# The first expert's raw w1 blocks 4 to 7, loaded behind the first queries into the buffers of the sums acc

## The chip, the cores and the metric

The kernel runs on one core of a Trainium2 chip. The metric is the device time of one execution in microseconds (us), the median of three runs. TensorE (PE) multiplies, VectorE (DVE), ScalarE (ACT) and GpSimd (POOL) work on tiles, and SyncE (SP) issues every DMA. Each of the five runs its own list of instructions in a fixed order, and an instruction that waits holds up all behind it on its engine.

## What is computed

A sparse attention over 4 batches, 8 heads and 768 positions of 64 numbers feeds a mixture of 4 experts. Each query sees the keys closer than 16 positions, and besides these 24 summaries of blocks of 32 (maximum of the keys, mean of the values).

```
k_sum = k.reshape(B, H, nb, block, D).max(axis=3)
v_sum = v.reshape(B, H, nb, block, D).mean(axis=3)
a = softmax([mask(scale * q @ k.T), scale * q @ k_sum.T + log(block)])
x = a @ concat(v, v_sum)                      # 3072 tokens of 512
h = np.maximum(x @ w1[e], 0.0)                # w1[e]: 512 x 1024
out += p[:, e:e + 1] * (h @ w2[e])            # w2[e]: 1024 x 512, p: probabilities of the domains
```

## The kernel before

**Tiles.** The 3072 tokens are eight blocks `tb` of 384. A block's attention is eight pieces `n` (96 queries times four heads). Pieces 0 to 7 make block 0 and have a path of their own, `first_tokens`, whose order is written out by hand with the keys `KEYS` and `STEPS`. From piece 8 on, a piece is: `load_piece` (its keys `kr` and its queries and values `qv`), `stage_a` (high and low parts: `ks`, `qs`, `v12`, `v3`), `scores` (`psc` on PE, its maxima on DVE, exponentials on ACT, in `ms`), `probs` (`rs`, `ms`, `aw`), `transposed` (a DMA that transposes `aw` into `awT`), `values` (`px` on PE, for two pieces one after the other) and `to_x` (`xh` on ACT, `xl` on DVE). Pieces 8 to 15 make block 1, and `xl` of pieces 14 and 15 is the last that block 1 waits for.

**Batches.** Pieces 16 and up belong to batch 1. For these `setup_k(1)` loads four chunks `kch1_0` to `kch1_3`, of which DVE takes block maxima into `ksr1`; `spread_k` then copies `ksr1` to `ks1` with four small DMAs. `setup_v(1)` does the same with `vch1_0` to `vch1_3` and sums `vsr1`, out of which ACT (`vs5`), PE (`pvs1`) and DVE make the summaries of the values. All eight chunks share two buffers (`chunk`), so that chunk 2 can be loaded only when DVE is through with chunk 0, and so on.

**Experts.** A block runs `plain_units`: for each of the eight 128-wide blocks `fc` of w1, 12 matmuls `ph` of 384 columns (`mm1`), then `hh` (ACT) and `hl` (DVE), and at the end the products `po` with w2 (`mm2`), 72 matmuls of 512 columns for a block of tokens, added to `acc` on DVE. A raw weight block of 256 KB is loaded to a buffer `wr`, ACT casts it to the high part (`wh` for w1), and POOL subtracts for the low part (`wl`); for w2 of the first expert DVE does (`w`), and the split w2 is stored to DRAM (`wd`) for later. Block 0 goes through experts 0 and 1, then block 1 through experts 1 and 0, and the rest follows. In names such as wr10_4, the digits are the 1 of w1, the expert, and `fc`.

**What sets the order.** In `first_tokens` engines keep the program's order. Behind that a scheduler places instructions by its own estimate of time. SP's list is one queue: a DMA whose buffer is not yet free, or whose data are not yet written, holds up all later DMAs.

**Buffers that the change touches.** `wr` has four buffers (lines 657 to 660). Before, w1 blocks 0 to 3 and then w2 blocks 0 to 3 of expert 0 take them in turn. w1 blocks 4 and 5 are asked for at the end of the hand-written list (key 99.0, lines 633 and 634), and so stand on SP behind the four stores of split w2, and behind the release of `wr` by the first splits of w2; blocks 6 and 7 are loaded when `plain_units` asks for them. `acc` (line 770) has six buffers of the same size; the first is written when the first product `po` of block 0 is done.

Of the kernel before, what the change touches and what calls it, by code (L numbers as in the profile page):

```python
# [8 lines left out]
F32 = mybir.dt.float32  # L9
# [7 lines left out]
P = 128  # L17
# [12 lines left out]
FC = DF // P  # L30
# [32 lines left out]
def attn_moe(ctx: ExitStack, tc: tile.TileContext, qvL, qv0, v0L, kD, kT, vT, w1L, w2L, dpL, cst, out):  # L63
# [21 lines left out]
    def pool(name, bufs=1, **kw):  # L85
        return ctx.enter_context(tc.tile_pool(name=name, bufs=bufs, **kw))
# [7 lines left out]
    sb = pool("sb")  # L94
# [302 lines left out]
    def first_tokens(units):  # L397
        kch = [sb.tile([P, S], F32, name=f"k0{hp}", tag="x", bufs=NX) for hp in range(4)]
        qvs = []
        for m in range(per):  # L400
            tag, bufs = ("w1", NW1) if m < 4 else ("x", NX)
# [8 lines left out]
        def at(key, f, *a):  # L410
            todo.append((key, len(todo), f, a))
# [5 lines left out]
        def load_qv(m):  # L417
            n = order[m]
            SP.dma_start(qvs[m], qv0[n // 2, n % 2])
# [196 lines left out]
        load_qv(2)  # L616
        load_qv(3)
        load_early(w1L, 0, "1")
        load_early(w1L, 1, "1")
        load_v(1)  # L620
        load_qv(4)
        load_qv(5)
        load_early(w1L, 2, "1")
        load_early(w1L, 3, "1")
        load_qv(6)
        load_qv(7)
        for fc in range(EARLY):
            at(KEYS[4 + fc], split_early, fc, "1", PL)
            at(KEYS[12 + fc], split_early, fc, "2", V)
            at(KEYS[12 + fc] - 1e3, load_early, w2L, fc, "2")  # L630
        at(-1.0, load_piece, per)
        at(-1.0, load_piece, per + 1)
        at(99.0, load_early, w1L, 4, "1")
        at(99.0, load_early, w1L, 5, "1")

        k_stats(0)
        k_stats(1)
# [16 lines left out]
    SLOW = 0.6  # L654
    US1, US2 = 0.175, 0.231

    def load_weights(src, e, fc, which):
        raw = sb.tile([P, 512], F32, name=f"wr{which}{e}_{fc}", tag="wr", bufs=4)
        SP.dma_start(raw, src[e, fc])
        return raw  # L660

# [22 lines left out]
    loaded, split = {}, {}  # L684

    def weights(src, e, fc, which, *a):
        if (e, fc, which) in stored and (e, fc, which) not in split:
            w = w2_part(e, fc)
            SP.dma_start(w.bitcast(F32), stored[e, fc, which])
            return w[:, 0, :], w[:, 1, :]  # L690
        if (e, fc, which) in split:
            return split.pop((e, fc, which))
        raw = loaded.pop((e, fc, which), None)
        return split_weights(raw or load_weights(src, e, fc, which), e, fc, which, *a)

    def load_early(src, fc, which):
        loaded[0, fc, which] = load_weights(src, 0, fc, which)

    def split_early(fc, which, *a):
        split[0, fc, which] = split_weights(loaded.pop((0, fc, which)), 0, fc, which, *a)  # L700
# [6 lines left out]
    def w1_operands(e, pr):  # L707
        ws = {w: w1_part(f"w1{w}{e}_{pr}") for w in WS}
        if (e, pr) in stored:
            for w in WS:  # L710
                SP.dma_start(ws[w].bitcast(F32), stored[e, pr][w])
            return ws
        r1, r2 = (load_weights(w1L, e, 2 * pr + j, "1") for j in range(2))
        a11, a12 = r1[:, 0:256], r1[:, 256:512]
        a21, a22 = r2[:, 0:256], r2[:, 256:512]
        stored[e, pr] = {}

        def parts(w, raw, lo):
            hi, low = ws[w][:, 0:256], ws[w][:, 256:512]
            A.copy(hi, raw)  # L720
            lo.tensor_tensor(low, raw, hi.bitcast(F32), op=ALU.subtract)
            stored[e, pr][w] = dram.tile([P, 512], F32, name=f"wd{w}{e}_{pr}")
            SP.dma_start(stored[e, pr][w], ws[w].bitcast(F32))

        parts("11", a11, PL)
        parts("22", a22, V)
        PL.tensor_tensor(a22, a21, a22, op=ALU.add)
        PL.tensor_tensor(a21, a11, a21, op=ALU.subtract)
        PL.tensor_tensor(a11, a22, a11, op=ALU.subtract)
        parts("s2", a11, V)  # L730
        parts("s1", a22, PL)
        parts("s3", a21, V)
        parts("12", a12, PL)
        PL.tensor_tensor(a12, a12, a11, op=ALU.subtract)
        parts("s4", a12, V)
        return ws

    acc, added = {}, {}
# [197 lines left out]
    at = 0  # L936
# [7 lines left out]
    EARLY = 4  # L944
    ahead = plain_units([0], 0, early=EARLY)
    first_tokens(ahead)
    pinned["load"] = False
    mixing()
# [97 lines left out]
```

## Time and profile before

| | us |
|---|---|
| median of three runs | 1178.3 (1177.82 to 1179.63) |
| the profiled execution | 1176.52 |
| its span, from first to last instruction | 1174.7 |
| PE busy | 1150.5 |
| DVE, ACT, POOL busy | 631.4, 541.2, 468.5 |

The page of the profile gives busy time by engine over the span; a timeline row has the start, the duration, the engine, the tiles written and read and the count, and in square brackets the idle time of the engine just before and what ended it. Starts of matmuls in a row are closer than their durations, since they are pipelined. The trace writes tiles without numbers: `psc` is the scores of any piece. A DMA's row on SP is its issue; it lands some us later.

### The profile page before, as it was taken

What the parts mean: (1) busy time and instruction counts of PE and PEld (TensorE: products, weight loads), DVE (VectorE), ACT (ScalarE), POOL (GpSimd) and SP (SyncE); (2) the same over time, 40 slices, a digit from 0 to 9 for tenths busy, and PEclk for the clock granted to TensorE, in tenths of its full rate; (3) what the DMA queues carried; (4) which work ended last, traced back from release to release, by engine and by line L of the source; (5) the groups of instructions that cost most, each with busy time, mean ns of one, the idle gap of its engine ahead of it and who ended that gap; (6) DMA issues with size and microseconds to landing.
All of it is one profiled execution on the core that took longest, in us unless ns stands there. A gap on an engine that the chain in (4) does not pass through costs nothing.

```text
span 1174.7 us, 20612 instructions
## 1 busy us (share of the span) xinstructions
PE 1150.5 (98%) x7188; PEld 1021.0 (87%) x7188; DVE 631.4 (54%) x1519; ACT 541.2 (46%) x1586; POOL 468.5 (40%) x578
## 2 busy tenths in 40 slices
PE   9898899999979999999999999999999999999998
PEld 7787789998968989898898989889898998989896
DVE  6778775555796837558586543535354222323131
ACT  5678667655666736546375443434343211202020
POOL 2398677846786737547265122221202000000000
PEclk9999999999999999999999999999999999999999
DMA  6699787957996878789963859678571556566531
GB/s 240 227 281 321 225 250 218 305 118 215 307 251 182 272 228 263 225 277 288 320 196 102 255 149 289 202 213 284 141 205 61 159 156 212 165 197 189 163 98 54
DMA packets 202329, 249.66 MB, mean 213 GB/s; under 512 B 82672, under 2 KB 118512, under 8 KB 202224
## 3 DMA queue, kind: packets, MB, share of 16 engines
q1 hardware_dynamic: 202224, 248.34, 69.6%
q8 instruction: 57, 0.93, 0.3%
q14 instruction: 48, 0.39, 0.1%
HBM read 174.22 MB, written 57.15 MB: 197 GB/s over the span
## 4 chain that ended last, share of the span: by engine, by line
PE 85%; DMA 4%; DVE 4%; POOL 3%; ACT 2%; issue 1%; SPq 1%; POOLq 0%; DVEq 0%; ACTq 0%
PE po L75 42%; PE phb L75 13%; PE pha L75 9%; PE ph L75 5%; PE phd L75 4%; PE phc L75 4%; PE psc L75 4%; PE px L75 3%; DMA vch<-in_vT 1%; PE pav L75 1%; DMA wr<-in_w2L 1%; DMA kch<-in_kT 1%; DVE ms L75 1%; SPq L75 1%; ACT ms L75 1%
## 5 line engine op out<-in xcount | busy, mean ns | idle before, releaser
L75 PE MATMUL po<-w,hh 128*128 128x512 f32 x1536 | 480.5, 394 | 0.0
L75 PEld LDWEIGHTS po<-w,hh 128*128 128x128 f32 x1536 | 284.2, 188 | 61.0
L75 PE MATMUL po<-w,hl 128*128 128x512 f32 x768 | 302.8, 397 | 0.0
L75 PEld LDWEIGHTS po<-w,hl 128*128 128x128 f32 x768 | 144.4, 188 | 31.5
L75 POOL TENSOR_TENSOR ks<-kr,ks 128x304 fp32r<-128x304 f32 x112 | 99.7, 897 | 176.8 <-ACT ks L75 160.5
L75 DVE CUSTOM_DVE_ANT_0 ms<-psc,c_sb 96x152 f32<-96x152 f32 x256 | 69.2, 306 | 104.6 <-PE psc L75 103.4
L75 PE MATMUL phb<-xh_t,w1s 128*128 128x384 f32 x384 | 114.2, 338 | 0.1
L75 ACT ACTIVATE ms<-ms,nb 96x152 f32<-96x152 f32 x256 | 104.3, 415 | 16.5 <-DVE nb L75 15.6
L75 PE MATMUL pha<-xh,w 128*128 128x384 f32 x384 | 110.7, 335 | 0.0
L75 DVE SCALAR_TENSOR_TENSOR acc<-po,pw,acc 128x512 f32<-128x512 f32 x72 | 51.9, 746 | 108.8 <-PE po L75 108.8
L75 PE MATMUL ph<-xh,wh 128*128 128x384 f32 x256 | 88.0, 347 | 4.8 <-ACT wh L75 3.7
L75 PE MATMUL ph<-xl,wh 128*128 128x384 f32 x256 | 87.4, 341 | 2.3 <-DVE xl L75 2.3
L75 DVE TENSOR_TENSOR aw<-ms,aw 96x512 f16<-96x512 f32 x112 | 77.2, 723 | 21.5 <-ACT aw L75 21.3
L75 PE MATMUL ph<-xh,wl 128*128 128x384 f32 x256 | 87.1, 341 | 1.2 <-POOL wl L75 1.2
L75 ACT CAST ks<-kr 128x304 fp32r<-128x304 f32 x112 | 48.1, 445 | 80.4 <-PE psc L75 62.9
L75 POOL TENSOR_TENSOR wl<-wr,wh 128x512 fp32r<-128x512 f32 x44 | 62.6, 1425 | 45.0 <-ACT wh L75 44.9
L75 ACT CAST aw<-ms 96x512 f16<-96x512 f32 x112 | 53.3, 523 | 56.3 <-issue 37.8
L75 POOL TENSOR_TENSOR qv<-qv,v 128x256 f32<-128x256 f32 x56 | 40.8, 739 | 78.2 <-ACT v L75 78.0
L75 ACT CAST v<-qv 128x256 bf16<-128x256 f32 x112 | 44.5, 405 | 59.2 <-PE px L75 40.8
L75 PEld LDWEIGHTS phb<-xh_t,w1s 128*128 128x128 f32 x384 | 70.8, 188 | 1.0 <-ACT phb L75 0.2
L75 PEld LDWEIGHTS pha<-xh,w 128*128 128x128 f32 x384 | 70.5, 188 | 0.3
L75 PE MATMUL phb<-xl_t,w1s 128*128 128x384 f32 x192 | 64.3, 335 | 0.0
(122 smaller groups left out, 2169.3 us busy)
## 6 DMA issues: line engine op xcount, KB each, us to landing
w<-wd SPq DMA_DIRECT2D x80, 512.0 KB, 4.4
w1s<-wds SPq DMA_DIRECT2D x112, 256.0 KB, 3.5
w<-wd SPq DMA_DIRECT2D x84, 256.0 KB, 3.4
wr<-in_w1L SPq DMA_DIRECT2D x76, 256.0 KB, 4.3
qv<-in_qvL SPq DMA_DIRECT2D x56, 320.0 KB, 4.4
wd<-w SPq DMA_DIRECT2D x32, 512.0 KB, 4.3
wds<-w1s SPq DMA_DIRECT2D x64, 256.0 KB, 2.7
kr<-in_kD SPq DMA_DIRECT2D x56, 256.0 KB, 3.7
```

Of the source, the lines that this page charges most:

```text
L75: ins = getattr(self.engine, name)(*a, **kw)
```

## The change

The raw w1 blocks 4 to 7 of expert 0 are now loaded in the hand-written list, right behind the last of the first queries (`qv0_7`), into four of the six `acc` buffers. The loads of blocks 4 and 5 at key 99.0 go away, and blocks 6 and 7 are no longer loaded when asked for. The splits, their engines and all matmuls stay.

```
@@ first_tokens
         load_qv(6)
         load_qv(7)
+        for fc in range(EARLY, FC):
+            load_early(w1L, fc, "1", "acc", 6)
         for fc in range(EARLY):
             at(KEYS[4 + fc], split_early, fc, "1", PL)
             at(KEYS[12 + fc], split_early, fc, "2", V)
             at(KEYS[12 + fc] - 1e3, load_early, w2L, fc, "2")
         at(-1.0, load_piece, per)
         at(-1.0, load_piece, per + 1)
-        at(99.0, load_early, w1L, 4, "1")
-        at(99.0, load_early, w1L, 5, "1")
@@ load_weights
-    def load_weights(src, e, fc, which):
-        raw = sb.tile([P, 512], F32, name=f"wr{which}{e}_{fc}", tag="wr", bufs=4)
+    def load_weights(src, e, fc, which, tag="wr", bufs=4):
+        raw = sb.tile([P, 512], F32, name=f"wr{which}{e}_{fc}", tag=tag, bufs=bufs)
@@ load_early
-    def load_early(src, fc, which):
-        loaded[0, fc, which] = load_weights(src, 0, fc, which)
+    def load_early(src, fc, which, *home):
+        loaded[0, fc, which] = load_weights(src, 0, fc, which, *home)
```

Since blocks 4 to 7 leave the rotation of `wr`, the scheduler places everything behind the first tokens anew. All five lists differ from before up to the middle of block 1's first pass (expert 1), and are the same in order after that. On PE, expert 0's `ph` of blocks 4 to 7 now stand in a row, and its `po` behind them, where before pieces of attention stood in between; at the entry to block 1, `pvs1` and all of piece 17's scores now stand ahead of the first `ph1_1`, where before they stood among them. Three more places follow, from the end of block 1's attention.

The first is SP's queue between the transposes of pieces 13 and 15. Before:

```order
L75 DMA_TRANSPOSE awT13_1513<-aw1_887 128x12x96
L143 DMA kch1_2_1725<-in_kT 128x768
L143 DMA kch1_3_1728<-in_kT 128x768
L75 DMA kr17_1790<-in_kD 128x4x128
L75 DMA qv17_1791<-in_qvL 128x640
L75 DMA wr11_2_2129<-in_w1L 128x512
L75 DMA_TRANSPOSE awT14_1691<-aw0_746 128x12x96
L75 DMA ks1_1731<-ksr1_1718 64x4x24 x4
L75 DMA_TRANSPOSE awT15_1779<-aw1_887 128x12x96
L143 DMA vch1_0_1869<-in_vT 128x768
L143 DMA vch1_1_1872<-in_vT 128x768
```

And with the change:

```order
L75 DMA_TRANSPOSE awT13_1513<-aw1_889 128x12x96
L143 DMA kch1_2_1725<-in_kT 128x768
L75 DMA kr17_1790<-in_kD 128x4x128
L143 DMA kch1_3_1728<-in_kT 128x768
L75 DMA qv17_1791<-in_qvL 128x640
L143 DMA vch1_0_1869<-in_vT 128x768
L75 DMA ks1_1731<-ksr1_1718 64x4x24 x2
L75 DMA_TRANSPOSE awT14_1691<-aw0_750 128x12x96
L75 DMA ks1_1731<-ksr1_1718 64x4x24 x2
L143 DMA vch1_1_1872<-in_vT 128x768
L143 DMA vch1_2_1875<-in_vT 128x768
L75 DMA qv18_1928<-in_qvL 128x640
```

The four loads of value chunks have moved ahead of awT15 (behind the rows shown come kr18, vch1_3 and then awT15; before, all four stood behind it), and awT14 now stands behind both later key chunks and in the middle of the copies to ks1.

The second is DVE, where the probabilities of piece 14 are made (ms14, then aw0). Before:

```order
L75 TENSOR_REDUCE ksr1_1718<-kch1_0_1719 128x24
L75 TENSOR_REDUCE ksr1_1718<-kch1_1_1722 128x24
L75 TENSOR_SCALAR rs14_1547<-rs14_1547 96x4
L75 RECIPROCAL rs14_1547<-rs14_1547 96x4
L75 TENSOR_TENSOR ms14_1545<-ms14_1545,rs14_1547 96x608
L75 TENSOR_TENSOR aw0_746<-ms14_1545,aw0_746 96x512
L75 TENSOR_TENSOR aw0_746<-ms14_1545,aw0_746 96x4x48
L75 TENSOR_REDUCE ksr1_1718<-kch1_2_1725 128x24
```

And with the change:

```order
L75 TENSOR_REDUCE ksr1_1718<-kch1_1_1722 128x24
L75 TENSOR_SCALAR rs14_1547<-rs14_1547 96x4
L75 RECIPROCAL rs14_1547<-rs14_1547 96x4
L75 TENSOR_REDUCE ksr1_1718<-kch1_2_1725 128x24
L75 TENSOR_TENSOR ms14_1545<-ms14_1545,rs14_1547 96x608
L75 TENSOR_REDUCE ksr1_1718<-kch1_3_1728 128x24
L75 TENSOR_TENSOR aw0_750<-ms14_1545,aw0_750 96x512
L75 TENSOR_TENSOR aw0_750<-ms14_1545,aw0_750 96x4x48
L75 TENSOR_REDUCE vsr1_1868<-vch1_0_1869 128x24
```

The reductions of key chunks 2 and 3 stood behind aw0 of piece 14 and now stand ahead of it.

The third is DVE at piece 15 (ms15, then aw1). Before:

```order
L75 TENSOR_REDUCE ksr1_1718<-kch1_3_1728 128x24
L75 TENSOR_SCALAR rs15_1704<-rs15_1704 96x4
L75 RECIPROCAL rs15_1704<-rs15_1704 96x4
L75 TENSOR_TENSOR ms15_1702<-ms15_1702,rs15_1704 96x608
L75 SCALAR_TENSOR_TENSOR xl1_0_1088<-px12_1619,xh1_0_1087 128x2x96
L75 SCALAR_TENSOR_TENSOR xl1_1_1090<-px12_1619,xh1_1_1089 128x2x96
L75 TENSOR_TENSOR aw1_887<-ms15_1702,aw1_887 96x512
L75 TENSOR_TENSOR aw1_887<-ms15_1702,aw1_887 96x4x48
L75 SCALAR_TENSOR_TENSOR acc0_1183<-po0_1_0_1675,pw_73,acc0_1183 128x512
```

And with the change, where the ISA rows are the maxima of piece 16's first scores:

```order
L75 TENSOR_SCALAR rs15_1704<-rs15_1704 96x4
L75 RECIPROCAL rs15_1704<-rs15_1704 96x4
L75 TENSOR_TENSOR ms15_1702<-ms15_1702,rs15_1704 96x608
L75 TENSOR_REDUCE vsr1_1868<-vch1_1_1872 128x24
L75 ISA ms16_1915,nb16_1916<-psc16_0_1918,c_sb_72 96x152
L75 ISA nb16_1916 96x1
L75 ISA ms16_1915,nb16_1916<-psc16_0_1918,c_sb_72 96x152
L75 ISA nb16_1916 96x1
L75 TENSOR_REDUCE vsr1_1868<-vch1_2_1875 128x24
L75 TENSOR_TENSOR aw1_889<-ms15_1702,aw1_889 96x512
L75 TENSOR_TENSOR aw1_889<-ms15_1702,aw1_889 96x4x48
```

Ahead of aw1 of piece 15 now stand the sums of value chunks 1 and 2 and half the maxima of piece 16; the `xl` of piece 12 and the sums acc0 to acc2 went further ahead.

## The prediction

> **What bounds the kernel now.** I read the page first, then a table by stages, then PE's timeline wherever PE was idle, then the lists of the engines that ended each wait. The page says that PE is the bound; the stages say where it is not full.
>
> ```profile
> span 1174.7 us, 20612 instructions
> PE 1150.5 (98%) x7188; PEld 1021.0 (87%) x7188; DVE 631.4 (54%) x1519; ACT 541.2 (46%) x1586; POOL 468.5 (40%) x578
> ```
>
> ```profile
> 40.00:60.00 20.00, 16.16 (x86) 14.55 (x85) 15.25 (x35) 11.90 (x29) 9.70 (x12) 0.91 0.85 293
> 60.00:80.00 20.00, 20.00 (x122) 16.91 (x121) 13.62 (x32) 14.81 (x45) 19.05 (x21) 1.00 0.90 260
> ```
>
> In each stage the columns are length, PE, PEld, DVE, ACT and POOL busy, PE's clock, the DMA share and GB/s. From 40 to 60 us PE is idle for almost 4 us and POOL for half the time; from 60 to 80 POOL is nearly full. Now PE's own rows, the idle time in brackets:
>
> ```profile
> 47.46 0.34 PE L75 MATMUL ph<-xh,wl 128*128 128x384 f32 x1
> 50.12 0.69 PE L75 MATMUL ph<-xh,wh 128*128 128x384 f32 x1 [2.33 <-ACT wh L75]
> ...
> 59.06 0.45 PE L75 MATMUL ph<-xh,wh 128*128 128x384 f32 x1 [1.34 <-ACT wh L75]
> ...
> 85.24 0.33 PE L75 MATMUL ph<-xh,wh 128*128 128x384 f32 x1
> ...
> 90.26 0.34 PE L75 MATMUL ph<-xh,wl 128*128 128x384 f32 x1
> ...
> 94.12 0.40 PE L75 MATMUL px<-awT,v 128*64 128x96 f16 x10 [1.42 <-DMA awT<-aw]
> ...
> 101.09 0.48 PE L75 MATMUL psc<-ks,qs 128*96 128x152 f32 x3 [0.60 <-POOL ks L75]
> 101.50 0.40 PE L75 MATMUL px<-awT,v 128*64 128x96 f16 x10
> ...
> 102.00 0.21 PE L75 MATMUL px<-awT,vs 120*64 120x96 f16 x2
> 103.39 0.44 PE L75 MATMUL ph<-xh,wl 128*128 128x384 f32 x1 [1.19 <-POOL wl L75]
> ...
> 111.38 0.49 PE L75 MATMUL psc<-ks,qs 128*96 128x152 f32 x4
> ...
> 113.23 0.63 PE L75 MATMUL po<-w,hh 128*128 128x512 f32 x2
> ...
> 118.08 0.62 PE L75 MATMUL po<-w,hh 128*128 128x512 f32 x2
> ...
> 118.77 0.83 PE L75 MATMUL psc<-ks,qs 128*96 128x152 f32 x8
> ...
> 129.82 0.40 PE L75 MATMUL px<-awT,v 128*64 128x96 f16 x10 [1.14 <-DMA awT<-aw]
> ...
> 134.24 0.44 PE L75 MATMUL ph<-xl,wh 128*128 128x384 f32 x1 [2.30 <-DVE xl L75]
> ...
> 142.00 0.49 PE L75 MATMUL psc<-ks,qs 128*96 128x152 f32 x4
> ...
> 143.96 0.49 PE L75 MATMUL psc<-ks,qs 128*96 128x152 f32 x4
> ...
> 149.73 0.49 PE L75 MATMUL pvs<-c_sb,vs 128*120 128x128 f32 x3
> ```
>
> The waits at 50.12 and 59.06 are for the high parts of blocks 4 and 6 of expert 0: what the change aims at. But 75 us later, at 134.24, PE waits again, for `xl` of pieces 14 and 15: block 1 cannot begin before its attention ends. So up to there two chains run side by side, the experts on block 0 and the attention of block 1, and the later one sets when PE goes on. Soon behind this point the lists of all engines are in the same order in both kernels; I take whatever shift stands there to reach the end.
>
> **The loads and splits of blocks 4 to 7.** Before, blocks 4 and 5 leave SP at 44.12; now all four do behind the last of the first queries, ahead of the w2 loads, where they cost SP four issues of 0.5 to 1 us and nothing waits for it closely:
>
> ```profile
> 44.12 2.00 SPq L75 DMA_DIRECT2D wr<-in_w1L  x2
> ```
>
> ```profile
> 50.15 1.46 POOL L75 TENSOR_TENSOR wl<-wr,wh 128x512 fp32r<-128x512 f32 x1 [14.51 <-ACT wh L75]
> ```
>
> ```profile
> 49.45 1.24 ACT L75 CAST wh<-wr 128x512 fp32r<-128x512 f32 x2 [1.13 <-DMA wr<-in_w1L]
> ```
>
> POOL had waited 14.51 us for block 4. That wait takes in four low parts (1.46 us, so 6 us at most). PE's 2.33 and 1.34 us go; three casts of 0.62 us (the row for ACT has two) now stand among the first tokens' work on ACT and may give back up to 1 us, an estimate for the two that stand ahead of work that PE waits for. So the experts' chain gains 2.7 to 3.7 us, and with the pieces of attention placed later in PE's list also the waits of 1.42, 0.60 and 1.19. None of it counts unless the attention of block 1 ends earlier too.
>
> **The attention chain, up to piece 13.** The milestone that I use is the transpose of piece 13 on SP:
>
> ```profile
> 112.08 1.69 SPq L75 DMA_TRANSPOSE awT<-aw  x1
> ...
> 119.26 1.54 SPq L75 DMA_TRANSPOSE awT<-aw  x1
> 121.89 2.61 SPq L75 DMA_DIRECT2D ks<-ksr  x4
> 126.44 1.31 SPq L75 DMA_TRANSPOSE awT<-aw  x1
> 127.80 1.30 SPq L143 DMA_DIRECT2D vch<-in_vT  x2
> ```
>
> These are awT13, awT14, the copies to ks1, awT15, and the first value chunks. In PE's new list, between the first `ph` of block 4 and the end of piece 13's scores, stand 144 `ph`, 85 `po`, six pieces of `psc` and four of `px`. From the rows above a `ph` takes 0.173 us (29 steps from 85.24 to 90.26), a `po` 0.231 (21 steps from 113.23 to 118.08), a `psc` about 0.8 and a `px` about 0.7: 24.9 + 19.6 + 4.8 + 2.8 = 52.1 us. Without any wait, from 47.8 (the end of the row at 47.46), that ends at 99.9, where before it ended at 101.6 (row 101.09). From the end of its scores to its transpose a piece took 10.5 us for 13, 7.4 for 14 and 6.8 for 15. So awT13 lies between 106.7 and, with no gain, 112.1. With the mean gap of 8.2, and with the waits of 1.42 and 0.60 for attention coming back elsewhere, since the pieces are now later in PE's list, I take 110.0: 2.1 us earlier.
>
> **From awT13 to block 1.** Here the new places on SP and DVE count. The durations on DVE:
>
> ```profile
> 115.81 0.79 DVE L75 TENSOR_TENSOR ms<-ms,rs 96x608 f32<-96x608 f32 x1
> 117.33 1.87 DVE L75 TENSOR_TENSOR aw<-ms,aw 96x512 f16<-96x512 f32 x2 [0.73 <-ACT aw L75]
> 119.12 0.94 DVE L75 TENSOR_REDUCE ksr<-kch 128x24 f32<-128x768 f32 x1
> ...
> 124.02 2.36 DVE L75 TENSOR_TENSOR aw<-ms,aw 96x512 f16<-96x512 f32 x2 [0.20 <-ACT aw L75]
> ...
> 132.02 0.95 DVE L75 TENSOR_REDUCE vsr<-vch 128x24 f32<-128x768 f32 x1 [3.67 <-DMA vch<-in_vT]
> 133.83 0.61 DVE L75 SCALAR_TENSOR_TENSOR xl<-px,xh 128x192 fp32r<-128x192 f32 x2
> ```
>
> A chunk issued at 127.80 is reduced at 132.02, 4.2 us later. Over the whole run the key chunks land after (shortest, median, longest):
>
> ```profile
> DMA to landing us min/median/max: 3.4/5.4/6.5
> ```
>
> Before: awT13 to awT14 7.2 us, to awT15 another 7.2, to PE's restart 7.8; 22.2 in all.
>
> With the change, awT14 waits for aw0 of piece 14, and that stands on DVE behind the reductions of key chunks 2 and 3. Chunk 2 is issued behind awT13: 1.7 (issue) + 4.2 (landing) + 0.94 + 0.79 (ms14) + 0.94 + 1.87 (aw0) = 10.4 us in place of 7.2. By the shortest and the median landing it is 9.6 to 11.6.
>
> awT15 waits for aw1 of piece 15, behind the sums of value chunks 1 and 2. Chunk 1 leaves SP behind awT14 and the second half of the ks1 copies: 1.5 + 1.3 + 4.2 + 0.94, then half of piece 16's maxima (0.5), 0.94 and aw1 (2.36) = 11.7 us in place of 7.2 (10.9 to 12.9).
>
> Block 1's `xl` now stands on DVE behind the other maxima of piece 16 (0.5), chunk 3 (0.94), rs16 and ms16 (1.4 from the rows) and aw0 of piece 16 (2.4), then 0.6 of its own: 5.8 us if nothing waits on ACT, up to 8, since the exponentials of piece 16 stand there behind casts of piece 18. I take 7.0; before it was 7.8. The wait of 3.67 for the value chunk ahead of `xl` is gone, because it has been taken earlier.
>
> The sum is 10.4 + 11.7 + 7.0 = 29.1 us, so PE goes on at 110.0 + 29.1 = 139.1 and not at 134.24: 4.9 us later. Against it, piece 17's scores (rows 142.00 and 143.96) and `pvs` (149.73) are already done then: 0.32 + 0.32 + 0.45 = 1.1 us off PE. Net: 3.8 us more. On the profiled execution (1176.52 = 1174.7 + 1.8 outside the span) that is 1180.3; on the median, 1.8 above it, 1178.3 + 3.8 = 1182.1.
>
> [...]
>
> **Rivals.** (1) The attention chain keeps its old pace: chunk loads land under DVE's other work, and block 1 starts at 134.24 as before. For it speaks that key chunks cost DVE no wait before (row 119.12 has none); against it, that they now stand directly ahead of aw0. Then only the 1.1 us counts: 1177.2, no change. A part of a later start could also be won back at the next places where PE waits for attention:
>
> ```profile
> 332.90 0.40 PE L75 MATMUL px<-awT,v 128*64 128x96 f16 x10 [1.32 <-DMA awT<-aw]
> ```
>
> Chance of both 0.27. (2) Faster: POOL is the true pace of the attention. The stage from 60 to 80 speaks for it, 19.05 of 20 busy; then the four low parts that left it (5.8 us at 1.46 each) move awT13 to 106.3, and if the steps to the restart also keep to 22.2 us, PE goes on at 128.5; with the 1.1, 6.8 us faster: 1171.5. It decides once awT13 plus these steps comes to under 133.0 (134.24 + 1.1 - 2.4). Against it: POOL's new list has low parts of expert 1 in the places that became free. Chance 0.13. (3) The change does not do what it says: block 4's `ph` needs the PSUM bank of block 0, which `hl` frees on DVE, and a split of w2 whose load has just been issued now stands ahead of that `hl`. Then PE's first wait stays. But PE has time to spare until 134, so the end is as forecast, with perhaps 1 us more for the attention: 1183.1. Chance 0.05.
>
> **How the numbers follow.** The forecast has the remaining 0.55. Its own range: awT13 at 106.7 with the shortest steps (9.6 + 10.9 + 5.8) restarts at 133.0, or 2.3 us faster with the 1.1; awT13 at 112.1 with the longest (11.6 + 12.9 + 8.0) at 144.6, 9.3 us slower. That is 1176.0 to 1187.6; I take 1175.5 to 1187.0, which leaves out rival 2 and the last of the slow end. About 0.2% (2.4 us) is what a measurement of this kernel can tell from no change. Faster by more: rival 2 and a little, 0.14. Within: rival 1 and the lower part of the forecast, 0.31. Slower: 0.55.
>
> **What would show it.** Right: the waits for `wh` at 50 and 59 us gone; POOL's 14.5 us wait cut up; on DVE new waits for key and value chunks right ahead of aw; awT13 to awT14 and awT14 to awT15 over 10 us each; one long wait of PE ahead of block 1's first `ph`, ended by `xl`, near 139 us. Wrong: a restart before 133, or a shift there that has shrunk by 400 us. The step that I trust least is awT13 at 110.

## The result, and the profile after

The changed kernel is slower: 1184.84 us (median of six runs, 1183.15 to 1188.16) against 1178.06 of the kernel before beside it, 6.8 us; ratio 1.0063, 95% interval 1.0045 to 1.0080. In a second series, 1186.51 against 1177.32: 1.0078, 1.0062 to 1.0094. The profiled executions are 1186.26 and 1176.52 us, 9.7 apart. The forecast was 1182.1 with a range of 1175.5 to 1187.0: right in sign, 2.7 us short in size.

The longest of PE's waits in the changed kernel up to the end of block 1, with the scores of piece 13 (107.08) and the first `xl` product of block 1 (149.19):

```profile
49.92 0.45 PE L75 MATMUL ph<-xh,wh 128*128 128x384 f32 x1 [0.64 <-DVE hl L75]
...
88.01 1.56 PE L75 MATMUL psc<-ks,qs 128*96 128x152 f32 x8 [1.98 <-POOL qs L75]
...
107.08 0.91 PE L75 MATMUL psc<-ks,qs 128*96 128x152 f32 x8
...
133.68 0.61 PE L75 MATMUL px<-awT,v 128*64 128x96 f16 x10 [7.38 <-DMA awT<-aw]
...
142.35 0.60 PE L75 MATMUL psc<-ks,qs 128*96 128x152 f32 x2 [4.40 <-ACT ks L75]
144.89 0.61 PE L75 MATMUL px<-awT,v 128*64 128x96 f16 x10 [1.94 <-DMA awT<-aw]
...
149.19 0.46 PE L75 MATMUL ph<-xl,wh 128*128 128x384 f32 x1
...
358.70 0.61 PE L75 MATMUL px<-awT,v 128*64 128x96 f16 x10 [5.19 <-DMA awT<-aw]
```

The waits of 2.33 and 1.34 us for `wh` at 50 and 59 us are gone; 0.64 is left, for `hl`. In their place PE waits for the attention of block 1, most of all for awT14 (at 133.68), awT15 (144.89) and the keys of piece 17 (142.35). Block 1 starts at 149.19, not 134.24: 14.95 us later. SP shows where that came from (rows of awT9, block 1's weights, the first key chunks, awT13, awT14, awT15):

```profile
81.91 1.30 SPq L75 DMA_TRANSPOSE awT<-aw  x1
...
111.36 2.08 SPq L75 DMA_DIRECT2D wr<-in_w1L  x3
114.46 0.90 SPq L143 DMA_DIRECT2D kch<-in_kT  x2
117.19 1.44 SPq L75 DMA_TRANSPOSE awT<-aw  x1
...
130.24 1.31 SPq L75 DMA_TRANSPOSE awT<-aw  x1
...
141.50 1.29 SPq L75 DMA_TRANSPOSE awT<-aw  x1
```

And DVE, the reductions of key chunks 0 and 3 and of value chunks 1 and 2:

```profile
120.55 0.95 DVE L75 TENSOR_REDUCE ksr<-kch 128x24 f32<-128x768 f32 x1 [3.42 <-DMA kch<-in_kT]
...
127.86 0.95 DVE L75 TENSOR_REDUCE ksr<-kch 128x24 f32<-128x768 f32 x1 [1.33 <-DMA kch<-in_kT]
...
136.84 0.95 DVE L75 TENSOR_REDUCE vsr<-vch 128x24 f32<-128x768 f32 x1 [1.19 <-DMA vch<-in_vT]
...
139.14 0.95 DVE L75 TENSOR_REDUCE vsr<-vch 128x24 f32<-128x768 f32 x1 [0.89 <-DMA vch<-in_vT]
```

The waits at 127.86 and 139.14 stand directly ahead of aw of pieces 14 and 15, as forecast. The longest, 3.42 us for chunk 0, stands earlier, ahead of the maxima of piece 14.

The stages, of before and then of after:

```profile
100.00:120.00 20.00, 18.22 (x139) 15.55 (x138) 19.13 (x42) 13.38 (x41) 16.07 (x16) 1.00 1.08 320
120.00:160.00 40.00, 36.29 (x251) 32.45 (x249) 31.14 (x75) 26.60 (x81) 32.03 (x34) 0.96 0.74 203
```

```profile
100.00:120.00 20.00, 20.00 (x162) 16.38 (x161) 12.20 (x32) 13.70 (x43) 17.23 (x18) 1.00 1.03 270
120.00:160.00 40.00, 24.27 (x184) 21.84 (x183) 32.20 (x82) 24.72 (x78) 22.50 (x27) 0.74 0.64 162
```

From 100 to 120 us DVE has 12.2 us of work where it had 19.1: the attention that feeds it is late. From 120 to 160 PE is idle for 15.7 us, and its mean clock is 0.74.

Not all of the 14.95 us reaches the end. Two waits of before are gone, and the long wait for attention that ends block 1 is 0.36 shorter. In the kernel before these were

```profile
235.38 0.44 PE L75 MATMUL ph<-xh,wh 128*128 128x384 f32 x1 [1.16 <-DVE hl L75]
...
349.95 0.61 PE L75 MATMUL px<-awT,v 128*64 128x96 f16 x10 [5.55 <-DMA awT<-aw]
```

and the 1.32 at 332.90 in the prediction. With the 1.1 us of PE work that stands ahead of the restart, as forecast, and 1.6 us that before lost to a slow clock behind its restart (0.96 over 40 us, 0.50 from 136 to 138; an estimate, 0.04 of 40), 14.95 - 1.16 - 1.32 - 0.36 - 1.1 - 1.6 = 9.4, against 9.7 between the two executions. The agreement is not exact: at the long wait the shift is 8.75 (358.70 less 349.95), 0.7 below this sum, and about 1 us comes back behind it; neither was followed.

### The profile page after: what moved, and what is told of

Its sections match the earlier page's. It is cut to its first block, busy times and chain, and to the rows that moved or that the text cites. A ratio compares the mean times of both kernels' runs of the same rounds, so it can differ in the third digit from the quotient of the medians.

```text
span 1184.4 us, 20613 instructions
## 1 busy us (share of the span) xinstructions
PE 1153.4 (97%) x7188; PEld 1023.6 (86%) x7188; DVE 623.8 (53%) x1519; ACT 542.6 (46%) x1586; POOL 465.9 (39%) x578
## 4 chain that ended last, share of the span: by engine, by line
PE 84%; DMA 5%; POOL 3%; DVE 3%; ACT 2%; issue 2%; SPq 1%; POOLq 0%; DVEq 0%; ACTq 0%
PE po L75 41%; PE phb L75 13%; PE pha L75 8%; PE ph L75 6%; PE phd L75 4%; PE phc L75 4%; PE psc L75 4%; PE px L75 2%; DMA kch<-in_kT 1%; DMA vch<-in_vT 1%; DMA wr<-in_w1L 1%; PE pav L75 1%; SPq L75 1%; DMA awT<-aw 1%; POOL qs L75 1%
## 5 line engine op out<-in xcount | busy, mean ns | idle before, releaser
L75 DVE TENSOR_TENSOR aw<-ms,aw 96x512 f16<-96x512 f32 x112 | 71.7, 674 | 20.7 <-ACT aw L75 20.6
L75 POOL TENSOR_TENSOR wl<-wr,wh 128x512 fp32r<-128x512 f32 x44 | 59.5, 1357 | 42.4 <-ACT wh L75 41.9
L75 PEld LDWEIGHTS psc<-ks,qs 128*96 128x96 f32 x448 | 54.3, 170 | 15.1 <-POOL qs L75 7.3
```

The source lines that it names most:

```text
L75: ins = getattr(self.engine, name)(*a, **kw)
```

## The experiments

Twelve runs follow, one of them the changed kernel again, each beside the kernel before on the same chip. The changed kernel is the base unless something else is said. In the first four, "theory 1" is the prediction's: the new order is the price, and the chunk sums ahead of aw are a part of it.

**v_later: value chunks half a step later.**

```
-        steps += [(k - 2.0, setup_k, b), (k - (0.5 if b == 1 else 1.0), setup_v, b)]
+        steps += [(k - 2.0, setup_k, b), (k - (0.0 if b == 1 else 1.0), setup_v, b)]
```

> The changed kernel with one number altered: the value chunks of batch 1 are set up half a step later, so that on DVE none of their sums stands ahead of aw1 of piece 15 and on SP none of their loads ahead of awT14. Theory 1 (the new order is the price, the chunks a part of it): awT14 to awT15 falls from 11.3 us to about 7.5; awT15 to PE's restart grows from 7.7 to about 8.5, since the value chunks now stand ahead of xl; restart near 146 us in place of 149.2, and about 2.5 us less than the changed kernel, 1182.3. Theory 2 (aw1 of piece 15 is late because its scores are late, and the chunk sums lie in that wait): awT14 to awT15 stays at 11, and the time within 1 us of the changed kernel, 1184 to 1186.

Measured: 1185.12 us, ratio 1.0061 (1.0040 to 1.0082). SP has awT14 and awT15 at

```profile
130.49 1.33 SPq L75 DMA_TRANSPOSE awT<-aw  x1
...
138.64 1.50 SPq L75 DMA_TRANSPOSE awT<-aw  x1
```

so the step is 8.15 us in place of 11.26, and block 1 starts 8.6 us behind it, at 147.26; both as expected. The time did not follow. By the long wait that ends block 1 (359.08, changed kernel 358.70) the 1.9 us are gone; but this trace reached the first product of block 4 at 53.27, 3.35 us later than the changed kernel's, so one trace of each can't say where.

**keys_behind: the key chunks behind awT14 as well.**

```
-        steps += [(k - 2.0, setup_k, b), (k - (0.5 if b == 1 else 1.0), setup_v, b)]
+        steps += [(k - (2.2 if b == 1 else 2.0), setup_k, b), (k - (0.0 if b == 1 else 1.0), setup_v, b)]
```

> The changed kernel with two numbers altered: values as in v_later, and the key chunks of batch 1 a fifth of a step earlier in the list of steps, by which the scheduler puts all four of their loads on SP behind awT14 and none of their sums on DVE ahead of aw0 of piece 14; chunks 0 to 2 stand ahead of aw1 of piece 15 instead. Theory 1: awT13 to awT14 falls from 13.05 to about 7.3 us, awT14 to awT15 stays near 11 (1.5 of issue, three more issues, 4.2 of landing, a sum, aw1); restart near 143 us; piece 17's scores and pvs are behind it again, so that some 4.5 us are gained on the changed kernel: about 1180.3. Theory 2: awT13 to awT14 stays over 11 us and the time at 1184 to 1186.

Measured: 1188.58 us, ratio 1.0106 (1.0086 to 1.0126): the slowest of all. And yet the chain did what theory 1 says, on SP awT13 to awT15,

```profile
116.06 1.30 SPq L75 DMA_TRANSPOSE awT<-aw  x1
...
121.74 1.28 SPq L75 DMA_TRANSPOSE awT<-aw  x1
...
132.72 1.88 SPq L75 DMA_TRANSPOSE awT<-aw  x1
```

5.7 us in place of 13.05, and block 1 starts 9.6 us earlier than in the changed kernel. PE, from that start to the long wait:

```profile
139.59 0.52 PE L75 MATMUL ph<-xl,wh 128*128 128x384 f32 x1
...
153.74 0.44 PE L75 MATMUL ph<-xh,wh 128*128 128x384 f32 x1 [1.18 <-DVE hl L75]
...
164.58 0.73 PE L75 MATMUL po<-w,hh 128*128 128x512 f32 x2 [3.63 <-DVE hl L75]
...
362.05 0.61 PE L75 MATMUL px<-awT,v 128*64 128x96 f16 x10 [4.35 <-DMA awT<-aw]
```

From start to long wait it takes 222.5 us, the changed kernel 209.5. 6.9 of the 13 are new waits (1.18 and 3.63, and for attention 1.03 at 174.97 and 1.09 at 346.22): the sums and the attention of piece 16 that DVE no longer did ahead of block 1 now stand among block 1's `hl`. Some 2.3 more are the scores of pieces 16 and 17 and `pvs`, which PE had done while it waited. The remaining 4 us or so, a part of it slow clock (0.97 from 150 to 200 us, 1.00 in the changed kernel), were not followed. So an earlier restart is worth nothing by itself when the work is only pushed behind it.

**keys_early: the key chunks ahead of their trouble.** The same line with 2.5 for 2.2.

> The changed kernel with two numbers altered: values as in v_later, and the key chunks half a step earlier, so that two of their loads stand ahead of awT12 and two ahead of the loads of block 1's weights behind it; no sum of a chunk stands directly ahead of aw0 of piece 14 or aw1 of piece 15 with a load just issued. Theory 1: both steps, awT13 to awT14 and awT14 to awT15, come to 7 to 8.5 us, awT13 stays within 2 us of 117.2, restart 140 to 142, time 1176.5 to 1179.5, about level with the kernel before. Theory 2: steps of 11 to 13 us stay, time 1184 to 1186.

Measured: 1185.13 us, ratio 1.0070 (1.0055 to 1.0085). awT14 comes 6.3 us after awT13, awT15 12.1 after awT14 (at 136.04), and block 1 starts at 146.71. The first step came even shorter than expected, the second did not. Against what the edit was to do, a value chunk's sum still stands on DVE directly ahead of aw of piece 15 and waits for its load, behind maxima of piece 16 that wait 0.78 us for their scores:

```profile
133.68 0.95 DVE L75 TENSOR_REDUCE vsr<-vch 128x24 f32<-128x768 f32 x1 [1.50 <-DMA vch<-in_vT]
```

With three kernels theory 1 has fallen as far as the chunks go: the waits stand there, but they are not what the time hangs on. What all three share with the changed kernel is awT13, at 116 to 118 us.

**late_home: the acc buffers without the early load.**

```
-        for fc in range(EARLY, FC):
-            load_early(w1L, fc, "1", "acc", 6)
...
+        for fc in range(EARLY, FC):
+            at(99.0, load_early, w1L, fc, "1", "acc", 6)
```

> Blocks 4 to 7 go into the acc buffers as in the changed kernel, but are loaded at the place where the kernel before loaded blocks 4 and 5. Theory 1, second part (awT13 is late since the raw buffers, no longer held by blocks 4 to 7, let expert 1's weights be loaded and split ahead of the attention): the order is nearly that of the changed kernel, awT13 comes at 115.5 to 119 us, the restart at 147 to 151, time 1183 to 1188. Theory 3 (the early loads are the price, by their traffic among the first queries and by ACT's casts among the first tokens): awT13 is back at 111 to 113, the restart below 138, time 1177 to 1180.

Measured: 1186.93 us, ratio 1.0088 (1.0073 to 1.0103). awT13 comes at 119.65, block 1 starts at 147.76, and a wait of 3.49 us for `wh` of block 4 is back. Theory 3 in this form is out: with the loads late the attention is as late. So what makes the attention late comes with the place of the raw blocks, not with the time of their loads. That they leave the four raw buffers to expert 1 was the next thing to look at.

**low_dve: expert 1's low parts off POOL.** From here on "theory 2" is a new one, formed from POOL's list: how many low parts `wl` (1.3 us each) stand there ahead of `qs` of a piece. (The edit holds for expert 1 in blocks 0 and 1.)

```
-                w1[fc] = weights(w1L, e, fc, "1", PL)
+                w1[fc] = weights(w1L, e, fc, "1", V if e == 1 and len(tbs) == 1 else PL)
```

> The changed kernel, with the low parts of expert 1's first-layer blocks taken on DVE in place of POOL while block 0 is worked on. By this the scheduler's order for pieces 9 to 15 and for the chunks of batch 1 comes back close to that of the kernel before (value chunks behind awT15, key chunks 2 and 3 behind awT13), while the early loads and the acc buffers stay. Theory 2 (with the raw buffers free, expert 1's weights are split on POOL and ACT ahead of the attention; that order is the price): awT13 at 110 to 113 us, both steps behind it 7 to 9, restart at 134 to 138, time 1175 to 1179. Theory 3 (the start is the price: awT8 is 4.9 us later than before by the loads and by where piece 8 stands, and the rest follows from it): awT8 stays near 71, awT13 at 116 or later, restart over 142, time 1183 to 1186.

Measured: 1177.23 us, ratio 0.9990 (0.9976 to 1.0004): all of the loss is back. SP, awT8, awT9, awT13:

```profile
72.77 1.86 SPq L75 DMA_TRANSPOSE awT<-aw  x1
...
76.70 1.30 SPq L75 DMA_TRANSPOSE awT<-aw  x1
...
112.10 1.70 SPq L75 DMA_TRANSPOSE awT<-aw  x1
```

awT8 is even later than in the changed kernel (71.20), and 6.4 later than in the kernel before (66.35); awT9 is 5.2 earlier than in the changed kernel and 0.9 earlier than before. So theory 3 is out here too: the lateness is not made ahead of awT8. awT14 comes at 118.96 and awT15 at 125.40, steps of 6.9 and 6.4, and block 1 starts at 132.90:

```profile
132.90 0.69 PE L75 MATMUL ph<-xl,wh 128*128 128x384 f32 x1 [1.38 <-DVE xl L75]
```

It also bears on what the waits at 50 and 59 us were worth: here they are gone, but for 0.83 at 50.08, PE waits for `xl` again ahead of block 1 (1.38 us, before 2.30), and the kernel takes as long as the one before, to within 0.24%. That the waits were worth nothing is not shown by this alone, since the move to DVE has a price of its own, as the control shows.

**before_low_dve: the control.** The same edit in the kernel before.

> The control to low_dve: the kernel before with the same move of expert 1's low parts to DVE. If the move is worth something in itself, it shows here too: 1172 to 1175. If it only mends the order that the change made, the time is within 2 us of the kernel before, and theory 2's reading of low_dve stands.

Measured: 1180.43 us, ratio 1.0026 (1.0016 to 1.0036), 3.1 us slower; a little outside what was expected. The move is no gain in itself, so what low_dve wins back, 9.3 us against the changed kernel in the same series (1186.51), comes from mending its order. In this control block 4 begins at 53.33, awT9 comes at 79.98, awT13 at 117.42 and block 1 starts at 138.65: awT13 is about as late as in the changed kernel, for less than half of the loss.

**two_acc: half of it.**

```
-        for fc in range(EARLY, FC):
+        for fc in range(EARLY, EARLY + 2):
             load_early(w1L, fc, "1", "acc", 6)
```

> The changed kernel with only blocks 4 and 5 loaded early into acc buffers; blocks 6 and 7 go through the raw buffers at their own time, as before. Theory 2: with two raw buffers held for longer, expert 1's weights come later, awT13 at 111 to 114 us, the wait of about 1.3 for block 6 stays, time 1177 to 1181. Theory 3: half the early loads, half the price, awT8 near 69, time 1180 to 1182.

Measured: 1181.64 us, ratio 1.0038 (1.0025 to 1.0051), just above what theory 2 gave and within theory 3's 1180 to 1182. Theory 3's sign did not come, though: awT8 is at 66.90, level with the kernel before, and not near 69. Nor did theory 2's: awT13 was to come at 111 to 114. awT9 is early (76.74), but awT13 comes at 122.22, later than in any other, and block 1 starts at 140.50. Here the lateness is made at piece 13, whose scores PE reaches only at 114.17, behind waits of 1.30 us (at 99.98) and 0.95 (at 104.51) and a long stretch of slow clock. PE's stage from 100 to 120 us:

```profile
100.00:120.00 20.00, 18.42 (x96) 15.84 (x97) 14.45 (x37) 13.88 (x42) 14.96 (x15) 0.74 1.08 270
```

The rows of `ph` last 0.52 us, 0.32 apart, from 106.09 to 108.66, and 0.34, 0.18 apart, at 113.27; at the half speed that these show, a mean clock of 0.74 over 20 us is an estimate of some 10 us of it. Where in the order this begins was not followed further.

**after_again: the changed kernel a second time.**

> The changed kernel unaltered, beside the others on the same chip, to see how far two profiled executions of it stand apart ahead of the first block 4 product, where no order differs. All theories: 1184 to 1186; the first block 4 product within 2 us of 49.9, and awT13 as far behind it as in the first trace, 67.3 us, to within 1 us.

Measured: 1186.51 us. The first product of block 4 at 49.59, awT13 65.9 us behind it (first trace 67.3), awT13 to awT14 14.4, to awT15 10.3, restart at 149.49. The 65.9 lies outside the 1 us that was expected, and awT9 comes at 79.62, 2.3 us earlier than in the first trace. Over the changed kernel and the versions that keep its early loads of all four blocks, whose hand-written order up to the first product of block 4 is the same, this product begins between 48.81 (keys_behind) and 53.27 us (v_later). So a time read from one trace holds to some 2 us, and better when taken from that product.

**low_first, low_last, low_odd: which low parts.** The line of low_dve with `and fc in (0, 1, 2, 3)`, `and fc in (4, 5, 6, 7)` or `and fc % 2`.

> The changed kernel, with only blocks 0 to 3 of expert 1's low parts on DVE, as long as one block of tokens is worked on. In POOL's list 8, 8, 9, 10 and 11 low parts then stand ahead of the queries qs of pieces 9 to 13 (changed kernel: 10, 12, 13, 15, 16; kernel before: 8, 10, 11, 12, 14). Theory 2a (the price is paid early: POOL waits in order for loads of expert 1 that come late, 1.4 us and 3.3 us, with qs of pieces 10 and 11 behind it): both waits go, awT11 comes at 94 to 97 us, awT13 at 110 to 113, time 1176 to 1180. Theory 2b (the price is POOL's time, so many low parts ahead of a piece): the same by this kernel; low_last tells them apart.

> As low_first, but blocks 4 to 7 on DVE. Ahead of qs of pieces 9 to 13 stand 10, 12, 12, 12 and 12 low parts: up to piece 10 as many as in the changed kernel, at piece 13 one more than in low_first. Theory 2a (early waits): the waits of 1.4 and 3.3 us stay, awT10 comes at 91 to 93 us and awT13 at 114 to 117, time 1182 to 1185. Theory 2b (POOL's time up to piece 13): awT13 within 2 us of that of low_first, time within 2 us of it.

> As low_first, but every second block (1, 3, 5, 7) on DVE; 9, 10, 10, 11 and 12 low parts ahead of qs of pieces 9 to 13. It lies between the two: by theory 2a one of the two early waits stays, awT13 at 112 to 115 us, time 1178 to 1183; by theory 2b within 2 us of low_first and low_last. If DVE, which is 19 of 20 us busy from 80 to 120 us in low_dve, is what keeps low_dve from being faster than the kernel before, this one or low_first is faster: 1172 to 1176.

Measured: 1179.61 (ratio 1.0023, 1.0010 to 1.0035), 1183.99 (1.0058, 1.0037 to 1.0079) and 1181.33 us (1.0038, 1.0024 to 1.0051). Theory 2b falls: at piece 13 low_first and low_last differ by one low part, and in time by 4.4 us. Theory 2a gives the times but not the reason: its waits do not go with them. POOL in low_first and in low_last:

```profile
79.06 1.27 POOL L75 TENSOR_TENSOR wl<-wr,wh 128x512 fp32r<-128x512 f32 x1 [5.29 <-ACT wh L75]
```

```profile
76.51 1.29 POOL L75 TENSOR_TENSOR wl<-wr,wh 128x512 fp32r<-128x512 f32 x1 [0.24 <-ACT wh L75]
```

The fast one has a wait of 5.29 us for a load, the slow one 0.24. Of POOL's list, what goes with the time is how many low parts stand ahead of `qs` of piece 9, and when awT9 comes. That is theory 2c; as theory 2a expected, low_odd (9 ahead of piece 9) lies between them. Neither it nor low_first is faster than low_dve, so there is no sign that DVE, with 19 of 20 us busy there, is what keeps low_dve from gaining.

**first_two: two operations.** The line of low_dve with `and fc < 2 and tbs == [0]`.

> The changed kernel, with two operations moved: the low parts of blocks 0 and 1 of expert 1, on DVE in place of POOL in block 0. They are the two that stand in POOL's list ahead of qs of piece 9 in the changed kernel (10 low parts there, 8 in the kernel before, 8 here); the order of all later pieces and of batch 1's chunks comes back close to the kernel before with them. Theory 2c (what counts is how many low parts stand ahead of pieces 9 and 10, since the lateness of piece 9 is carried on to the end of the chain): awT9 at 76 to 78.5 us, awT13 at 111 to 114, restart at 133 to 138, time 1176 to 1179.5. Rival (many low parts must leave POOL, as in low_dve): awT13 at 115 or later, time 1181 to 1184.

Measured: 1179.31 us beside 1178.03, ratio 1.0007 (0.9994 to 1.0019). SP, awT9 and awT13, and PE's start of block 1:

```profile
78.90 1.71 SPq L75 DMA_TRANSPOSE awT<-aw  x1
...
112.59 1.25 SPq L75 DMA_TRANSPOSE awT<-aw  x1
```

```profile
136.15 0.69 PE L75 MATMUL ph<-xl,wh 128*128 128x384 f32 x1
```

awT14 and awT15 come 8.7 and 8.0 us after one another. Two of POOL's operations, 2.6 us of work, bring back all but some 1.3 us. POOL around `qs` of piece 9, in the changed kernel and in first_two:

```profile
61.80 1.31 POOL L75 TENSOR_TENSOR wl<-wr,wh 128x512 fp32r<-128x512 f32 x1
...
63.88 1.32 POOL L75 TENSOR_TENSOR wl<-wr,wh 128x512 fp32r<-128x512 f32 x1
65.28 2.04 POOL L75 TENSOR_TENSOR qs<-qv,qs 64x384 fp32r<-64x384 f32 x1
```

```profile
65.11 1.01 POOL L75 TENSOR_TENSOR qs<-qv,qs 64x384 fp32r<-64x384 f32 x1
...
69.64 2.00 POOL L75 TENSOR_TENSOR wl<-wr,wh 128x512 fp32r<-128x512 f32 x1
```

first_two is done with these `qs` at 66.1, though its block 4 began 2 us later (51.97); the changed kernel at 67.3.

And yet POOL's time is not what holds piece 9. In the changed kernel PE begins the scores of piece 9 at 69.43 without a wait, 2.1 us after these `qs` are done. The traces show the lateness at two other places. One is PE's list: without any wait between, these scores begin 19.5 us behind the first product of block 4 in the changed kernel, and 17.0 in low_dve, low_first and first_two. The other is ACT's: in the changed kernel the cast `wh` of a block of expert 1 stands ahead of the exponentials of piece 9 (rows `ms<-ms,nb`) and waits for its load, while DVE has the maxima done at 70.99; in first_two it stands behind them.

```profile
74.78 0.62 ACT L75 CAST wh<-wr 128x512 fp32r<-128x512 f32 x1 [3.01 <-DMA wr<-in_w1L]
...
76.03 0.42 ACT L75 ACTIVATE ms<-ms,nb 96x152 f32<-96x152 f32 x1
```

```profile
73.49 0.42 ACT L75 ACTIVATE ms<-ms,nb 96x152 f32<-96x152 f32 x1
...
75.43 0.60 ACT L75 CAST wh<-wr 128x512 fp32r<-128x512 f32 x1
```

Together that is 2.5 + 3.0 = 5.5 us; taken from the first product of block 4, awT9 is 32.0 us behind it in the changed kernel and 26.6 in low_dve, 5.4 apart. In the changed kernel's second trace the cast waits 1.17 us: 3.7 by this sum, 3.4 measured. In low_last it waits 1.84 ahead of the exponentials; in low_first the waits for such loads (0.73 and 1.58) come behind them. So theory 2a had the right kind of wait on the wrong engine. This is read from the traces; no run moved this cast alone.

Eight of the kernels in one table (the counts are of POOL's lists; the first product of block 4, awT9, awT13 and the start of block 1 are of one trace each; us is the median, beside a kernel before at 1176.3 to 1178.1, and the ratio is to that):

| kernel | `wl` ahead of qs9, qs10 | block 4 | awT9 | awT13 | block 1 | us | ratio |
|---|---|---|---|---|---|---|---|
| before | 8, 10 | 50.12 | 77.62 | 112.08 | 134.24 | 1178.06 | 1 |
| low_dve | 8, 8 | 50.08 | 76.70 | 112.10 | 132.90 | 1177.23 | 0.9990 |
| first_two | 8, 9 | 51.97 | 78.90 | 112.59 | 136.15 | 1179.31 | 1.0007 |
| low_first | 8, 8 | 49.94 | 76.55 | 112.10 | 139.30 | 1179.61 | 1.0023 |
| low_odd | 9, 10 | 49.07 | 78.25 | 115.37 | 144.24 | 1181.33 | 1.0038 |
| two_acc | 8, 10 | 48.67 | 76.74 | 122.22 | 140.50 | 1181.64 | 1.0038 |
| low_last | 10, 12 | 52.29 | 82.96 | 116.77 | 145.99 | 1183.99 | 1.0058 |
| changed kernel | 10, 12 | 49.92 | 81.91 | 117.19 | 149.19 | 1184.84 | 1.0063 |

two_acc stands apart: its piece 9 is in time and its piece 13 is not; the control before_low_dve is like it. Of the others, the four with awT13 at 112 to 113 us are the fast ones. Taken from block 4, awT9 is 26.6 to 27.5 us behind it with eight low parts, 29.2 with nine and 30.7 to 32.0 with ten; awT13 is 60.6 to 62.2 behind it with eight and 64.5 to 67.3 with nine or ten.

No version beats both kernels by more than its interval; low_dve is level with the kernel before.

**What stays open.** That moving the two low parts ahead of piece 9 brings nearly all of the loss back is shown by first_two. What moves with them, PE's, ACT's and DVE's order (the scheduler sets them all from the same estimate), was not separated by a run, since an order can't be held while one operation leaves it; that PE's place for the scores and ACT's cast carry the 5 us at awT9 rests on the traces. What makes piece 13 late in two_acc and in the control was not followed. Nor was it followed why v_later's earlier restart was used up. A fifth raw buffer, which would test the rotation itself, was not tried.

## Why the prediction was right, and where it failed

**The waits at 50 and 59 us: right.** They go, 0.64 stays for `hl` (the mechanism of rival 3, at a fraction of its price), and "None of it counts unless the attention of block 1 ends earlier too" fits low_dve, where PE waits for `xl` again, though the control's 3.1 us could hide a small gain there.

**awT13 at 110.0, the step trusted least: failed.** It came at 117.19, outside its own bounds of 106.7 to 112.1. The scores of piece 13 were to end at 99.9 without a wait; they ended at 108.0. Of the 8.1 us, 1.5 are a later first product of block 4 (ready at 49.3, not 47.8), 3.3 are five waits of PE ahead of them (1.98 for the queries of piece 11, and 0.46, 0.43, 0.23 and 0.23), and 1.7 the slow clock behind the longest (0.50 from 88 to 91 us and 0.79 from 91 to 92); of the 1.6 left over, 0.64 is the wait for `hl` at 49.92. From there to awT13 it was 9.2, not 8.2. The step took PE's list for what sets the pace, and let the waits come back with 2.0 us only. Against rival 2 the prediction said that POOL's list "has low parts of expert 1 in the places that became free". Ahead of each of pieces 9 to 13 there stood in fact two to three low parts more than before, and first_two shows that with two of them moved nearly all of the loss goes. The prediction did not ask what else moves up with them: ACT's casts, which wait for loads ahead of the exponentials of piece 9, and PE's `po` ahead of its scores.

**awT13 to awT14, 10.4: right in kind, short in size.** 13.05 in one trace, 14.4 in the other. The forecast had chunk 2 as the one that DVE waits for. The first wait, 3.42 us, was for chunk 0: its load left SP only at 114.46, behind three loads of block 1's weights and the load of piece 16's queries.

**awT14 to awT15, 11.7, and to the restart, 7.0: right.** 11.26 and 7.69. One sign did not come: there is no long wait of PE that `xl` ends. PE waits for awT14, the keys of piece 17 and awT15, and then runs `pvs` and scores at a granted clock of 0.50 (145 to 149 us) up to 149.19.

**What the chunk steps are worth: wrong.** The sum counted 3.2 and 4.5 us of these steps as time. keys_behind took 7.4 us out of the first and was slower by 2 to 4 us (1188.58 against 1186.51 and 1184.84). While awT13 is late, DVE has that work left to do in any case; ahead of block 1 it stands in one long wait, behind the restart it stands in `hl`. With awT13 in time a step can cost something: low_first has awT13 where low_dve has it, 12.1 us from awT14 to awT15 (11.7 forecast) in place of 6.4, and takes 2.4 us more by the medians, 3.9 by the ratios. But a chunk is little of that step: the one value chunk whose sum stands ahead of aw of piece 15 makes DVE wait 0.46 us (at 125.93), after a wait of 3.60 for `xh` of ACT (at 124.85), which itself waits 2.48 for a load of queries (at 123.57).

**The sum: +3.8 forecast, +6.8 in the medians.** The restart was 14.95 us later, not 4.9; 7.2 of the difference are awT13, 2.7 awT13 to awT14. The step that carries the shift of the restart to the end unchanged failed too: of 14.95 us, 8.75 are left at the long wait that ends block 1, which is in part the shrinking that was to be a sign of being wrong. That the time came within the range is luck: a restart three times as late as forecast was offset by what was given back later, the 1.1 that the sum had, the two waits of before that vanished (rival 1 had named the one at 332.90), and the slow clock of before, which no term had.

**The price of a load.** The sum took 4.2 us for a chunk, from one value chunk of before. The list of DMA issues of the changed kernel has medians of 4.2 us from issue to landing for value chunks and 5.9 for key chunks, by which the term was 1.7 us short for these:

```profile
kch<-in_kT SPq DMA_DIRECT2D x12, 384.0 KB, 5.9
vch<-in_vT SPq DMA_DIRECT2D x12, 384.0 KB, 4.2
```

## What to carry to other kernels

Here the buffers that became free were used at once, by whatever the scheduler had next: ask which work moves up, and count on each engine's list what then stands ahead of the work that the end waits for. Do this at the first piece of a chain, not the last: lateness made at piece 9 showed as PE's waits at pieces 14 to 17, where mending them gained nothing. Look for operations that wait for a load (here ACT's casts of weights) in front of ready work of the chain. A wait removed in front of a later wait is worth what the later one allows; here no gain was seen.

## What the runs showed of the hardware

PE ran at half speed behind short waits. In low_dve three waits of 0.56, 1.15 and 1.23 us, 2.94 in all, stand within 5 us; behind them the eight `psc` show 1.56 us (0.83 at 74.92) and rows of a single `ph` 0.52 us, 0.32 apart, and from 85.80 on 0.33 us, 0.17 apart. The mean clock is 0.91 from 80 to 100 us and 1.00 from 100 to 120.

```profile
78.66 0.40 PE L75 MATMUL px<-awT,v 128*64 128x96 f16 x10 [0.56 <-DMA awT<-aw]
...
80.52 0.40 PE L75 MATMUL px<-awT,v 128*64 128x96 f16 x10 [1.15 <-DMA awT<-aw]
...
82.45 1.56 PE L75 MATMUL psc<-ks,qs 128*96 128x152 f32 x8 [1.23 <-POOL qs L75]
...
84.22 0.52 PE L75 MATMUL ph<-xh,wl 128*128 128x384 f32 x1
...
85.80 0.33 PE L75 MATMUL ph<-xl,wh 128*128 128x384 f32 x1
```

What the clock follows in these rows no run shows. In the changed kernel the mean clock is 0.95 from 120 to 130 us, 0.50 up to 145 and 0.56 up to 150: half from 129.0 us, 2.7 us into the wait of 7.38, to 149.4. Waits of 0.49, 0.27, 4.40 and 1.94 us lie in between, with bursts of `px` and `psc`, so that the bursts ahead of the restart ran at half speed too (ten `px` 0.60 to 0.65 us; 0.40 and 0.38 at 106 us).
